# Hyena filter and maxout FFN: the products of the FFN beside the convolution in four column blocks of 32 in place of two of 64

## The chip, the cores and the metric

The kernel runs on one core of a Trainium2 chip. The time is the device time of one execution in microseconds; the kernel before took 2205.84 us, the median of three runs (2205.76 to 2206.69). The engines are called as the profile calls them: PE (TensorE, matrix products), PEld (PE's loads of the stationary operand), DVE (VectorE), ACT (ScalarE), POOL (GpSimd) and SP (SyncE, which issues DMAs).

## The reference

Two blocks follow one another, all in float32.

```
# hyena filter: x, v [4, 12544, 128], pos_emb [12544, 64], w1 [64, 64], w2 [64, 128]
h_filt = (np.maximum(pos_emb @ w1, 0.0) @ w2) * np.exp(-0.01 * pos)[:, None]
Uf = np.fft.rfft(x * v, n=2 * S, axis=1)
Hf = np.fft.rfft(h_filt, n=2 * S, axis=0)
y = x * np.fft.irfft(Uf * Hf[None, :, :], n=2 * S, axis=1)[:, :S, :]
# maxout FFN on the 50176 rows of y: moe_w1, moe_w2, moe_w3 [128, 768], moe_w_out [768, 128]
h = np.maximum(np.maximum(y @ moe_w1, y @ moe_w2), y @ moe_w3)
out = h @ moe_w_out
```

## The kernel before

The long convolution is done as a Fourier transform in two steps, with tables of constants: the 12544 positions are 98 blocks of 128, and a transform over the blocks (90 frequencies, `N1`) is followed by one within a block. Channels or positions lie on the partitions, and all of these transforms are matrix products on PE. The product with the filter's spectrum is element by element, on DVE, ACT and POOL; the way back is a second pair of transforms.

The work has three parts in time.

- First the filter, the weights and the convolution of batch 0, up to about 281 us of the span.
- Then the loop over `tiles[:LAST]`: 96 FFN tiles, 32 for each of the batches 0, 1 and 2. A tile is 392 positions (4 of the 128 within a block, by 98 blocks). Beside the tiles of batch b runs the convolution of batch b + 1; `conv_steps` lays its steps out over slots, six slots a tile, and `run` issues them at the end of each slot. This part ends at about 1792 us.
- Last the 32 tiles of batch 3, two at a time, with a scheme that needs fewer products, and no convolution beside them.

What belongs to a tile in the second part:

- `t_load` fetches the tile's spectrum from DRAM by DMA, `t_sums` forms two sums of it (L818, L820).
- `t_last`, the **last stage** of the inverse transform, makes 8 products of 49 columns, for 4 positions and the two halves of the 98 blocks: the sums `even` and `zt` in turn, times the table `f4p`, all into one bank. The bank is read by DVE, which multiplies with x (L839) into `gt`. It is called in one of the slots 2 to 4 of the tile before.
- `up` makes one of six chunks of 128 of the hidden layer: two products of 392 columns, `w_sb[1]` and `w_sb[2]` times `gt`, into two banks of `hps`. ACT takes the Relu of the first (L849), DVE the maximum with the second (L852). (The third matrix is folded in beforehand, into differences of the weights and a direct product `lin`.)
- `down` adds one chunk's product `wo_sb` times `hid` into the bank `ops`, two chunks after `up`; with the first chunk also `lin` times `gt`. After the sixth ACT copies the bank (L865) and POOL stores it by DMA (L867).

Beside them, of the convolution: `u_products` (L451, pieces of 49 rows by 64 columns, 90 columns wide) and `g_quarter` (L549 and L559, pieces of 64 rows by 64 columns, 128 columns wide). A `g_quarter` treats one step of the way forth and one of the way back, three steps apart, and between them stands a chain on the other engines: ACT's copy `eo` (L571), DVE's sums `cb` (L574), ACT's swap (L589, L590), DVE's products with the filter (L593, L598), POOL's add (L601) and DVE's `xs` (L605), which L559 reads. Those pieces are written out in the code and don't depend on the block's width.

The order on every engine is the order in the code (`manual_schedule`); buffers and data are waited for by semaphores.

`up`, `down` and `t_last` all send their products through one helper, `halves_mm` (L169 is its call of `matmul`). It cuts the stationary operand into blocks of `block[0]` columns, each of which fills as many partitions of the output, and sends the whole moving operand through each:

```
    block = [64]

    def halves_mm(out, lhsT, rhs, start, stop):
        w = block[0]
        for h in range(0, P, w):
            nc.tensor.matmul(out[h:h + w], lhsT[:, h:h + w], rhs,
                             start=start, stop=stop, skip_group_check=True)
```

In the trace every float32 matmul of the code stands as two records with a weight load each, here called two passes. A group's name gives rows and columns of the piece: `128*64` is 128 rows by a block of 64 columns, `90*64` the last stage's.

`block[0]` is 64 up to the end of the second part; the third part runs with 32 (its own products at L913 are cut in blocks of 32 by the code).

## Time and profile before

| | before |
|---|---|
| median of three runs | 2205.84 us (2205.76 to 2206.69) |
| the profiled execution | 2205.64 us |
| its span in the profile | 2203.9 us |
| granted clock of PE | 0.999 |
| busy in the span: PE, PEld, DVE | 2186.5, 1258.5, 1533.7 us |
| busy in the span: ACT, POOL | 1211.4, 1183.3 us |
| up products, 128*64 by 392 columns | 4616 records, 865.1 us busy |
| down products, 128*64 by 392 columns | 2304 records, 476.8 us busy |
| `lin` products, 128*64 by 392 columns | 384 records, 79.5 us busy |
| last stage, 90*64 by 49 columns, `zt` and `even` on `cps` | 1552 records each, 95.9 and 94.6 us busy |
| last stage of the third part, 90*32 by 49 columns | 960 records each, 24.1 and 24.2 us busy |

The busy time of a group is the time in which at least one of its records runs. Records overlap: blocks of columns work side by side, and the end of one pass lies over the start of the next, so the mean length of a record (494 ns for a wide one) is longer than the distance from pass to pass, and the distance between starts says what a pass costs.

### The profile page before, as it was taken

The numbers are of one execution on the slowest core, as the hardware profiler recorded it, in microseconds if no ns is written. First come the engines' busy times: TensorE is split into PE (matmuls) and PEld (weight loads), VectorE is DVE, ScalarE is ACT, GpSimd is POOL, SyncE is SP. The second block draws the span as 40 slices with busy tenths as digits, with TensorE's granted clock in tenths as the row PEclk, the third lists the DMA queues.
The fourth block names the chain that finished last, engine by engine and source line by source line (L and its number), as shares of the span: only waits on it lengthen the run. The fifth ranks groups of instructions, "written<-read, shape, count | busy, mean of one in ns | idle before, by whom it ended". The sixth has DMA issues, their size and how long they took to land.

```text
span 2203.9 us, 77207 instructions
## 1 busy us (share of the span) xinstructions
PE 2186.5 (99%) x31655; PEld 1258.5 (57%) x31655; DVE 1533.7 (70%) x3292; ACT 1211.4 (55%) x2223; POOL 1183.3 (54%) x1580
## 2 busy tenths in 40 slices
PE   9999999999999999999999999999999999999998
PEld 8988855555555555555555455555555545555565
DVE  5688966678888766668888766668878745454443
ACT  3699845466666555466666555456666522222222
POOL 1166568545544667535455566534545326666665
PEclk9999999999999999999999999999999999999999
DMA  8789999879999899789999899879999622222221
GB/s 200 184 262 318 302 181 206 170 196 247 248 245 246 209 189 178 155 193 243 245 245 251 212 193 175 171 172 244 242 251 241 179 75 59 65 71 69 59 59 24
DMA packets 491270, 411.62 MB, mean 187 GB/s; under 512 B 289379, under 2 KB 407901, under 8 KB 490917
## 3 DMA queue, kind: packets, MB, share of 16 engines
q1 hardware_dynamic: 443495, 274.33, 57.5%
q0 software_dynamic: 45936, 130.43, 20.9%
q8 instruction: 249, 4.08, 0.8%
q10 hardware_dynamic: 1486, 1.93, 0.4%
q14 instruction: 104, 0.85, 0.1%
HBM read 262.85 MB, written 84.68 MB: 158 GB/s over the span
## 4 chain that ended last, share of the span: by engine, by line
PE 93%; DVE 2%; POOL 2%; issue 1%; DMA 0%; ACT 0%; POOLq 0%; ACTq 0%; DVEq 0%
PE hps L169 46%; PE ops L169 20%; PE ops L913 6%; PE cps L169 4%; PE cps L549 3%; PE cps L451 3%; PE ps L178 3%; PE cps L559 3%; PE ps L169 2%; POOL xt L640 1%; PE last L169 1%; DVE ab L647 1%; PE ps L393 1%; DVE xs L639 1%; POOL specH L640 1%
## 5 line engine op out<-in xcount | busy, mean ns | idle before, releaser
L169 PE MATMUL hps<-gt,w_sb 128*64 128x392 f32 (+1 forms) x7672 | 1151.8, 494 | 1.8 <-DVE hid L852 1.0
L849 ACT ACTIVATE hid<-hps 128x392 f32<-128x392 f32 x768 | 382.4, 498 | 745.2 <-PE hps L169 726.9
L169 PEld LDWEIGHTS hps<-gt,w_sb 128*64 128x64 f32 (+1 forms) x7672 | 413.7, 126 | 454.5 <-issue 415.9
L852 DVE TENSOR_TENSOR hid<-hid,hps 128x392 f32<-128x392 f32 x768 | 428.5, 558 | 339.9 <-PE hps L169 321.4
L169 PE MATMUL ops<-hid,wo_sb 128*64 128x392 f32 x2304 | 476.8, 492 | 0.0
L601 POOL TENSOR_TENSOR cb<-cb,xs 128x512 f32<-128x512 f32 x135 | 178.2, 1320 | 358.3 <-DVE xs L598 349.8
L169 PEld LDWEIGHTS ops<-hid,wo_sb 128*64 128x64 f32 x2304 | 165.7, 137 | 213.5 <-issue 213.5
L574 DVE TENSOR_TENSOR cb<-cps,eo 128x512 f32<-128x512 f32 (+1 forms) x288 | 175.2, 650 | 78.0 <-ACT eo L571 76.9
L867 POOL DMA_DIRECT2D out_dram<-ot x96 | 77.1, 803 | 263.6 <-ACT ot L865 247.3
L589 ACT ACTIVATE xs<-cb 32x512 f32<-32x512 f32 x270 | 169.5, 628 | 21.9 <-DVE cb L574 13.1
L590 ACT COPY xs<-cb 32x512 f32<-32x512 f32 x270 | 166.3, 616 | 3.1
L605 DVE TENSOR_TENSOR xs<-cb 128x256 f32<-128x256 f32 x270 | 148.3, 598 | 7.3 <-POOL cb L601 7.3
L431 ACT COPY uT<-turned 113x512 uint16<-113x512 uint16 x180 | 125.9, 770 | 1.9 <-DMA turned<-planes 1.7
L388 POOL TENSOR_TENSOR ut<-ut 128x392 f32<-128x392 f32 x90 | 92.8, 1032 | 43.1 <-DMA ut<-in_vr_dram 42.9
L582 POOL DMA_DIRECT2D zd<-cb x135 | 93.8, 695 | 39.9 <-DVE cb L574 36.8
L169 PEld LDWEIGHTS cps<-f4p,even 90*64 90x64 f32 x1552 | 87.2, 138 | 35.9 <-issue 33.1
L777 POOL DMA_DIRECT2D xT<-in_x_dram x172 | 101.4, 605 | 4.6 <-DVE ab L647 3.1
L473 DVE TENSOR_TENSOR low<-high,cps 128x180 f32<-128x180 f32 x186 | 54.7, 336 | 68.9 <-ACT high L463 68.9
L938 POOL DMA_DIRECT2D out_dram<-o x120 | 72.6, 610 | 45.6 <-DVE o L931 44.5
L169 PE MATMUL cps<-f4p,zt 90*64 90x49 f32 x1552 | 95.9, 222 | 0.0
L415 POOL COPY planes<-ut 128x392 uint16<-128x392 uint16 x180 | 94.9, 561 | 0.0
L169 PE MATMUL cps<-f4p,even 90*64 90x49 f32 x1552 | 94.6, 220 | 0.0
(173 smaller groups left out, 3306.1 us busy)
## 6 DMA issues: line engine op xcount, KB each, us to landing
ht<-hd SPq DMA_DIRECT2D x264, 256.0 KB, 6.8
wt<-wq_const POOLq DMA_DIRECT2D x144, 256.0 KB, 5.6
zd<-cb POOLq DMA_DIRECT2D x135, 256.0 KB, 5.1
zt<-zd SPq DMA_DIRECT2D x384, 90.0 KB, 3.8
sq<-spec SPq DMA_DIRECT2D x528, 64.0 KB, 5.9
ut<-in_xr_dram SPq DMA_DIRECT2D x128, 196.0 KB, 4.0
ut<-in_vr_dram SPq DMA_DIRECT2D x128, 196.0 KB, 4.3
wt<-wt_const SPq DMA_DIRECT2D x90, 256.0 KB, 5.1
```

Source lines behind the costliest of these rows:

```text
L169: nc.tensor.matmul(out[h:h + w], lhsT[:, h:h + w], rhs, start=start, stop=stop, skip_group_check=True)
L415: nc.gpsimd.tensor_copy(w[:, h, :, :, 0:HB], a[:].bitcast(U16).rearrange("p s (m e h) -> p h s e m", e=2, h=2)[:, h])
L431: nc.scalar.copy(uts[u][0:HR, 8 * (u % 2):8 * (u % 2) + 8].rearrange("n s r t -> n (s r t)").bitcast(U16).rearrange("n (s r t h) -> n h s ...
L574: nc.vector.tensor_tensor(out=cb[:, a, lo:hi], in0=ps[:, lo:hi], in1=eo[:, lo:hi], op=op)
L589: nc.scalar.mul(xs[at:at + 32], xt[at + 32:at + 64], -1.0)
L590: nc.scalar.copy(xs[at + 32:at + 64], xt[at:at + 32])
L601: nc.gpsimd.tensor_tensor(out=xts[g], in0=xts[g], in1=xs[:], op=ALU.add)
L605: nc.vector.tensor_tensor(out=ab[:, q], in0=y[:, 0], in1=y[:, 1], op=(ALU.subtract, ALU.add)[q])
L777: eng.dma_start(xT[c * NG:(c + 1) * NG].rearrange("d i p n -> d (i p) n"), x[:, 4 * i:4 * i + 8, c, b, :])
L849: nc.scalar.activation(h[:], pa[:, 0:N], Relu)
L852: nc.vector.tensor_tensor(out=h[:], in0=h[:], in1=pb[:, 0:N], op=ALU.max)
L913: nc.tensor.matmul(ps[32 * q:32 * q + 32, 0:H2], w[:, m:m + 32], rhs[:, H2 * c:H2 * c + H2], start=start, stop=True, skip_group_check=True)
```

## The change

The width is set to 32 before the loop over the 96 tiles, not after it. So `up`, `down` and `t_last` send four blocks of 32 columns in the second part, too, each with its own weight load, where they sent two of 64. `t_last` runs 98 times in this loop, as it also makes the first two tiles of batch 3; `up` 577 times with the first chunk of batch 3; `down` for all 576 chunks, and `lin` 96 times. Products of the convolution, buffers, the other engines' instructions and the order of everything stay as they are. Line numbers between the two places rise by one.

```diff
             besides.setdefault((b - 1) * NT * NF + s, []).extend(steps)
+    block[0] = 32
     for n, (b, i) in enumerate(tiles[:LAST]):
         if i == 0:
             plan, pairs_from = plans[b]
...
     for l in late:
         down(*l)
     conv.close()
-    block[0] = 32
```

## The prediction

> **What bounds the kernel now.** I read the page first, then the busy time by stage, then the waits of PE inside the stage that the change touches.

> ```profile
> PE 2186.5 (99%) x31655; PEld 1258.5 (57%) x31655; DVE 1533.7 (70%) x3292; ACT 1211.4 (55%) x2223; POOL 1183.3 (54%) x1580
> ...
> PE 93%; DVE 2%; POOL 2%; issue 1%; DMA 0%; ACT 0%; POOLq 0%; ACTq 0%; DVEq 0%
> ```

> PE (TensorE) is busy 99% of the span and holds 93% of the chain that ended last. By stage (columns: PE, PEld, DVE, ACT, POOL, granted clock, DMA share, GB/s):

> ```profile
> 281.00:1792.00 1511.00, 1507.93 (x17676) 783.34 (x17672) 1122.33 (x2389) 892.27 (x1629) 799.71 (x1099) 1.00 0.94 210
> 1792.00:2203.90 411.90, 405.95 (x8178) 233.63 (x8176) 198.20 (x366) 105.79 (x224) 265.38 (x313) 1.00 0.23 58
> ```

> The first row is the stage of the change: FFN tiles of three batches beside the convolution of the next. The second is the last batch, which already uses blocks of 32; so one trace holds both block widths, at the same clock. PE's waits in the first stage:

> ```profile
> PE hps L169 <- DVE hid L852: 1.0, 1, 1.0
> PE hps L169 <- DVE gt L839: 0.7, 1, 0.7
> PE cps L559 <- DVE xs L605: 0.5, 2, 0.3
> ```

> Some 3 us in 1511: the stage is as long as PE's own work, and what the pieces of a product cost is what counts.

> **The last stage (t_last), 98 tiles.** Its products are 49 columns wide. With blocks of 64 (timeline of PE; start, length, instruction, count):

> ```profile
> 1206.35 0.27 PE L169 MATMUL cps<-f4p,even 90*64 90x49 f32 x4
> 1206.45 0.29 PE L169 MATMUL cps<-f4p,zt 90*64 90x49 f32 x4
> ...
> 1207.15 0.29 PE L169 MATMUL cps<-f4p,zt 90*64 90x49 f32 x4
> 1207.27 1.50 PE L169 MATMUL hps<-gt,w_sb 128*64 128x392 f32 x8
> ```

> With blocks of 32, in the last batch:

> ```profile
> 1854.71 0.27 PE L169 MATMUL last<-f4p,even 90*32 90x49 f32 x8
> 1854.80 0.27 PE L169 MATMUL last<-f4p,zt 90*32 90x49 f32 x8
> ...
> 1855.33 0.26 PE L169 MATMUL last<-f4p,zt 90*32 90x49 f32 x8
> 1855.42 0.83 PE L169 MATMUL hps<-gt,w_sb 128*32 128x392 f32 x8
> ```

> Eight products take 1207.27 - 1206.35 = 0.92 us by two blocks of 64 and 1855.42 - 1854.71 = 0.71 us by four of 32; the trace's starts in ns have medians of 0.920 (98 stages) and 0.706 (30 stages). One product is sent as two records for each block, 4 against 8, so the 32-wide pieces are twice as many and still quicker: 0.115 us a product becomes 0.088. [...] 96 tiles of three batches and the first two of the fourth get their last stage in this loop: 98 x 0.214 = **21.0 us less**. All of it is on PE, so on the path.

> [...]

> **The wide products.** Up and down products (392 columns) go from 4 records to 8. At 64, two ups and a down run 1204.37 to 1206.35, 0.66 us a product; at 32, 1859.72 to 1861.70 holds two ups and two half-wide products of the last batch (0.33 each), again 0.66 a full one. Median from pass to pass is 329 ns in both widths. Nothing saved, nothing added: **0**. The doubled weight loads lie under the products: the PEld rows below show 0.13 us of loading in each 0.33 at 32, 0.14 at 64; without that cover each would cost what the returns show, 0.02 to 0.05. ACT and DVE read the same banks in as many instructions; no DMA, SP or POOL instruction changes.

> **The weight loads after a change of shape.** When PE returns from the convolution's 64 x 64 pieces it starts empty, and the second load of the first up cannot hide (timeline of PEld):

> ```profile
> 1211.26 0.20 PEld L169 LDWEIGHTS hps<-gt,w_sb 128*64 128x64 f32 x4 [0.17 <-issue]
> 1211.65 0.14 PEld L169 LDWEIGHTS hps<-gt,w_sb 128*64 128x64 f32 x2 [0.19 <-issue]
> 1211.98 0.14 PEld L169 LDWEIGHTS hps<-gt,w_sb 128*64 128x64 f32 x2 [0.18 <-issue]
> ...
> 1792.13 0.16 PEld L169 LDWEIGHTS hps<-gt,w_sb 128*32 128x32 f32 x8 [0.61 <-DVE hid L852]
> 1792.49 0.13 PEld L169 LDWEIGHTS hps<-gt,w_sb 128*32 128x32 f32 x4 [0.20 <-issue]
> ```

> The second pass follows 0.39 us after the first, where 0.33 is usual (0.380 against 0.329 in ns); at the trace's one change into blocks of 32 (1792.13) it follows after 0.36 (0.353). So 0.027 less at each return. The order of work in the trace shows 118 visits to the convolution in this stage (72 of its products at L549 and L559, 46 of its transforms at L451), each with one return: 118 x 0.027 = **3.2 us less**. After a last stage the second pass is 15 ns late at 64 and 5 ns at 32; 95 such: **0.9 us less**. The one change from 64 to 32 at 1791.7 goes (0.431 against 0.329): **0.1 us less**.

> **The changes of shape themselves** (236, two a visit) stay as many, but are now from 128 x 32 to 64 x 64, which the trace doesn't show. Nearest rows, by starts in ns: 128 x 64 to 64 x 64 costs 0.100 and back 0.110; 128 x 98 to 98 x 64 and 128 x 64 to 128 x 32 cost 0.100; between 128 x 98 and 64 x 41, where rows and columns change at once, 0.095 to 0.100. I take no difference, as the last of these is the nearest in kind, with 12 ns either way on one half as bound (118 x 0.012 = 1.4 us). One more thing: after a return four blocks start 7 ns apart, so the last ends 20 ns after the first instead of 7, until a last stage closes them up again; the next change waits for it. Between 0 and 118 x 0.013 = 1.5; I take **1.0 us more**.

> **What is late next.** PE arrives earlier at the convolution's products, which read xs (DVE, L605). The chain behind it (ACT copies, DVE sums, POOL's add, L605) is in part of fixed length: from 482.83, where the visit ends, to 494.69 those engines hand over almost without a pause. Comparing L605's second half with the first pass that uses that group, visits leave 0.8 to 3 us, 0.2 to 0.5, 0.07 to 0.08, or, where no last stage lies between two visits, -0.09 to -0.02; down to -0.09 no pause of PE is seen, since the second half is read two passes later. About 57 of the gaps between visits hold one last stage and shrink by 0.24. If the chain didn't move at all, the visits at 0.08 would fall to -0.16 and lose some 0.07 us (about 10 of them, 0.7 us), the pause of 0.43 us at the end of the first two convolutions would grow by up to 0.24 each (0.5), and the dozen at -0.09 to -0.02 would lose the 0.03 of their return (0.3). Bounds: nothing, and 57 x 0.24 = 13.7; I take **1.5 us more**, by the measured slack.

> **The sum**: -21.0 - 3.2 - 0.9 - 0.1 + 1.0 + 1.5 = -22.7 us. The profiled execution took 2205.64 us (span 2203.9), 0.2 below the median of 2205.84; so 2182.9 on it and about 2183 for the median, 1.0% faster.

> **Rivals.**
> (a) The convolution's chain takes the gain back: nothing behind L605 moves with PE, and each gap gives up its 0.24. Then 13.7 in place of 1.5 is lost: 2195. For it: 11.9 us of nearly unbroken work between two visits. Against: that chain starts from PE's own visit, and most gaps have over 0.24 us to spare. 0.05.
> (b) A change of row and column size together is paid twice, 0.10 more on each of 236: +23.6, and the gain is gone, 2206.6, no difference. For it: the pair isn't in the trace. Against: the changes between 128 x 98 and 64 x 41 at the single price. 0.04.
> (c) Slower: under a DMA share of 0.94 (0.23 where the 32-wide stage was seen) the pieces don't overlap, and each costs what a 64-wide one does, 0.1175 / 4 = 0.029 us. The 784 products then take 8 x 0.029 = 0.235 us, not 0.1175: +92, less the 4 saved at the returns, plus 2.5: about 2296. It decides from about 0.015 us a piece, where the gain is gone. For it: twice the instructions have to come in while DMA is busy, 64 pieces more a tile. Against: up to 281 us the kernel ran 5807 matmul records (20.7 a us) at a DMA share of 0.86, where the changed stage would have 17676 + 10440 in about 1490 us (18.9 a us), and the convolution's 64 x 64 pieces, four side by side, keep 109 ns a pass at the full DMA load. 0.03. [...]
> That the change does nothing is excluded: the pieces of all three kinds go by the one helper, and the program's PE instructions change from 64 to 32 columns throughout this stage.

> **The numbers.** The forecast's mechanism has 0.88; its own range is 2179.2 (no stall, no skew, 1.4 off for the changes of shape) to 2190.5 (skew 1.5, half the bound of the stalls, 1.4). That holds 8 in 10 by itself, so the range is 2179 to 2191. Faster: forecast and (a), 0.93; about 0.2% (4.4 us) is what a measurement of this kernel can tell from no change. Same: (b), 0.04. Slower: (c), 0.03.

> **What would show it.** The groups of 90*64 pieces in this stage give way to 90*32 ones in twice the number, and a last stage to 0.71 us. The stage from 281 to 1792 ends near 1769, the last batch keeps its 412 us. The second pass after a return comes at 0.36. PE's wait for L605 stays below 2 us in sum; if it is 10, (a) is right. If the last pass before a visit and its first are more than 0.43 apart, (b); if the eight products take over 0.9 us, (c). Wide passes other than 329 ns would break the sum at the term I set to nothing.

## The result and the profile after

The changed kernel is slower: 2230.55 us, the median of four runs (2227.61 to 2234.29), against 2206.27 (2205.76 to 2207.26) of the kernel before on the same chip. The ratio is 1.0108 with a 95% interval of 1.0096 to 1.0119. The profiled execution took 2230.39 us, its span 2228.6.

The page's rows of engines and of the chain, and the one of PE's instruction queue, which is new to the reading (transfers, MB, share):

```profile
PE 2180.8 (98%) x42095; PEld 1234.7 (55%) x42095; DVE 1536.5 (69%) x3292; ACT 1213.0 (54%) x2223; POOL 1186.8 (53%) x1580
...
q8 instruction: 331, 5.42, 1.1%
...
PE 92%; DMA 3%; issue 2%; DVE 1%; ACT 1%; SPq 0%; ACTq 0%; POOL 0%; DVEq 0%; POOLq 0%
```

PE has 10,440 matmul records more, as foreseen, and yet 6 us less busy time (2186.5 before): the saving is there, and PE stands still for longer than it saved. (Of the chain's 3% of DMA, more than half lies ahead of the changed stage.) By stage, the changed one and the third part:

```profile
281.00:1815.00 1534.00, 1502.40 (x28172) 726.16 (x28167) 1124.59 (x2388) 894.23 (x1629) 803.40 (x1099) 1.00 0.95 207
1815.00:2228.60 413.60, 407.72 (x8204) 268.68 (x8196) 198.89 (x368) 106.27 (x225) 265.11 (x313) 1.00 0.23 59
```

Before, PE was idle for 3 us in the changed stage; now it is for 1534.00 - 1502.40 = 31.6. The last part is as it was. PE's waits in the changed stage:

```profile
PE hps L169 <- issue: 10.1, 6, 3.1
PE cps L549 <- issue: 6.1, 7, 1.6
PE cps L451 <- issue: 4.7, 2, 2.7
PE cps L559 <- issue: 3.7, 4, 1.5
PE cps L549 <- DMA sq<-spec: 1.5, 1, 1.5
PE cps L549 <- DVE hid L852: 1.2, 1, 1.2
...
PE cps L559 <- DVE xs L605: 0.5, 2, 0.2
```

Some 26 us of the idle time are "issue": PE waits for no semaphore that the profile shows. Two waits are new, for `sq` and for `hid`; what they are is said below. The wait for `xs`, which the prediction gave 1.5 us, has not moved.

**The part that came as forecast.** A last stage now, on PE's timeline:

```profile
1021.48 0.27 PE L169 MATMUL cps<-f4p,even 90*32 90x49 f32 x8
1021.57 0.27 PE L169 MATMUL cps<-f4p,zt 90*32 90x49 f32 x8
...
1022.10 0.27 PE L169 MATMUL cps<-f4p,zt 90*32 90x49 f32 x8
1022.19 1.50 PE L169 MATMUL hps<-gt,w_sb 128*32 128x392 f32 x16
```

That is 0.71 us, as in the last batch, at a DMA share of 0.95.

**What a pause looks like**, in the middle of a transform of the convolution:

```profile
426.53 0.84 PE L169 MATMUL ops<-hid,wo_sb 128*32 128x392 f32 x8
427.30 0.69 PE L451 MATMUL cps<-f1e,uT 49*64 49x90 f32 x23
430.66 1.91 PE L451 MATMUL cps<-f1e,uT 49*64 49x90 f32 x41 [2.67 <-issue]
```

23 of 64 pieces run, then nothing for 2.67 us, and the profile shows no semaphore that is waited for. The DMA records give the reason. PE's instructions come over queue q8, in 331 transfers of 16 KB (5.42 MB / 331). The trace holds 84,190 products and weight loads of PE and some 600 semaphore instructions, 256.2 for each of the 331 transfers: a transfer is a block of 256 instructions, 64 bytes each (16,384 / 256).

I counted PE's instructions in the program's order (four for each matmul of the code, and the semaphore instructions) up to each pause. The 13 longest of the changed stage all begin at the same place of 256, wherever in the work that is (0.79 to 0.82 of a block; the number depends on where the count begins, what matters is that it is the same each time), and all end 1.3 to 1.7 us after a q8 transfer has ended (here the transfer ran from 428.04 to 429.09). At none of the stage's 222 borders between blocks does PE go on sooner than 1.2 us after the end of the transfer that belongs there. So in these pauses PE stands at the border of an instruction block whose successor hasn't come.

Two of the 13 are the waits that the page puts down to `sq` and `hid`: they begin at such a border, too, and end 1.58 and 1.41 us after a transfer, though for `sq` the trace doesn't exclude that its data were late as well. One block is fetched ahead: by the array's time a transfer starts between 1.6 us before PE comes to the border before and 6.5 us after, in the median 1.6 us after.

Against each other, in us, worked out from the trace (time of a block: from border to border on PE; delay: from a border to the end of the next block's transfer, and 1.35 for what follows it, by the 1.3 to 1.7 above; how the semaphore instructions are counted in shifts single figures by up to half a microsecond):

| stage | time of a block: least, median | delay: median, a tenth over, longest |
|---|---|---|
| before, changed stage | 7.2, 10.6 | 3.3, 5.5, 7.6 |
| before, third part (blocks of 32, DMA share 0.23) | 4.0, 6.3 | 2.0, 3.3, 3.9 |
| after, changed stage | 3.6, 6.6 | 4.3, 7.0, 9.2 |

Before, even the shortest block lasted about as long as the longest delay, and in this stage nothing was seen of it. After, the two overlap. The transfer itself hardly differs (a median of 1.17 us in the changed stage, 1.09 in the third part before); what differs is how late it starts.

**The account.** I compared each stretch of equal work with the time that the fastest tenth of its kind takes, and summed the excess: 2.6 us before, 47.4 after. From the first wide product of the loop to the first narrow one of the third part it is 1521.8 us before and 1545.2 after: +23.4 = +44.8 of pauses - 21.4 of savings. In that excess lies a second thing. After four of the five longest pauses (2.24 to 3.61 us from start to start) PE's granted clock was halved for 3.41 us; the one of 2.95 us, up to 1012.85, was followed by the full clock. The first of the four:

```profile
330.25:331.67 1.42, 1.42 (x31) 0.91 (x35) 0.00 (x0) 0.46 (x1) 0.56 (x2) 1.00 1.07 245
331.67:335.08 3.41, 3.41 (x28) 1.09 (x21) 2.01 (x7) 0.50 (x1) 1.80 (x2) 0.50 1.27 170
335.08:340.00 4.92, 4.92 (x64) 1.94 (x60) 2.90 (x9) 3.39 (x7) 3.47 (x6) 1.00 1.04 229
```

The last column but two is the clock: 1.00, 0.50, 1.00. Wide passes at half the clock take 0.65 us in place of 0.33. The four stretches begin at 331.67, 430.66, 597.91 and 942.66 us, whole multiples of 3.413 us apart (29, 49 and 101). Half of 3.41 us, four times, is at most 6.8 of the 44.8 (one of the four began 0.44 us before its pause ended). The rest is pauses; of those the idle time of 31.6 us shows only what lies beyond the modelled ends of the last records. Counted another way, the 22 gaps of over 0.5 us between starts at block borders alone come to some 31 us.

### The profile page after: what moved, and what is told of

Its sections match the earlier page's. It is cut to its first block, busy times and chain, and to the rows that moved or that the text cites. A ratio compares the mean times of both kernels' runs of the same rounds, so it can differ in the third digit from the quotient of the medians.

```text
span 2228.6 us, 98087 instructions
## 1 busy us (share of the span) xinstructions
PE 2180.8 (98%) x42095; PEld 1234.7 (55%) x42095; DVE 1536.5 (69%) x3292; ACT 1213.0 (54%) x2223; POOL 1186.8 (53%) x1580
## 3 DMA queue, kind: packets, MB, share of 16 engines
q8 instruction: 331, 5.42, 1.1%
## 4 chain that ended last, share of the span: by engine, by line
PE 92%; DMA 3%; issue 2%; DVE 1%; ACT 1%; SPq 0%; ACTq 0%; POOL 0%; DVEq 0%; POOLq 0%
PE hps L169 45%; PE ops L169 19%; PE ops L913 6%; PE cps L549 3%; PE ps L169 3%; PE cps L169 3%; PE cps L451 3%; PE ps L178 3%; PE cps L559 3%; PE sps L1135 2%; PE last L169 1%; PE gps L1110 1%; PE ps L393 1%; DMA ht<-hd 1%; PE ps L355 1%
## 5 line engine op out<-in xcount | busy, mean ns | idle before, releaser
L169 PE MATMUL hps<-gt,w_sb 128*32 128x392 f32 x12288 | 1172.9, 494 | 12.0 <-issue 10.1
L852 DVE TENSOR_TENSOR hid<-hid,hps 128x392 f32<-128x392 f32 x768 | 428.6, 558 | 367.2 <-PE hps L169 350.4
L169 PEld LDWEIGHTS hps<-gt,w_sb 128*32 128x32 f32 x12288 | 404.8, 110 | 476.0 <-issue 426.4
L169 PE MATMUL ops<-hid,wo_sb 128*32 128x392 f32 x4608 | 497.5, 494 | 0.0
L169 PEld LDWEIGHTS ops<-hid,wo_sb 128*32 128x32 f32 x4608 | 156.0, 110 | 227.1 <-issue 224.4
L605 DVE TENSOR_TENSOR xs<-cb 128x256 f32<-128x256 f32 x270 | 148.6, 598 | 7.3 <-POOL cb L601 7.3
L549 PE MATMUL cps<-sq,wt 64*64 64x128 f32 x2160 | 90.3, 277 | 8.8 <-issue 6.1
L169 PEld LDWEIGHTS cps<-f4p,even 90*32 90x32 f32 x3104 | 76.2, 109 | 39.2 <-issue 30.4
L593 DVE TENSOR_TENSOR cb<-cb,ht 128x512 f32<-128x512 f32 x135 | 92.0, 682 | 3.1 <-ACT xs L590 3.1
```

The source lines that it names most:

```text
L169: nc.tensor.matmul(out[h:h + w], lhsT[:, h:h + w], rhs, start=start, stop=stop, skip_group_check=True)
L549: nc.tensor.matmul(ps[64 * a:64 * a + 64, at:at + D], w[64 * r:64 * r + 64, k, a, :], t[64 * r:64 * r + 64, k, :, a], start=(k == 0), stop ...
L605: nc.vector.tensor_tensor(out=ab[:, q], in0=y[:, 0], in1=y[:, 1], op=(ALU.subtract, ALU.add)[q])
L852: nc.vector.tensor_tensor(out=h[:], in0=h[:], in1=pb[:, 0:N], op=ALU.max)
```

## The experiments

Theory 1 is the supply of instructions, as above. Theory 2 is the rival: something in the width of 32, in the array or in the change between 128x32 and 64x64, that pauses now and then. Ratios are to the kernel before on the same chip, with 95% intervals.

**s1_cut_columns.** As many instructions for the wide products, with blocks of 64.

```diff
-        for h in range(0, P, w):
-            nc.tensor.matmul(out[h:h + w], lhsT[:, h:h + w], rhs,
+        for at in range(0, n, c):          # c = n // 2 for n > 256 in the loop
+            for h in range(0, P, w):
+                nc.tensor.matmul(out[h:h + w, at:at + c], lhsT[:, h:h + w], rhs[:, at:at + c],
```

> Blocks stay 64 wide; instead every wide product of the loop (up, down, lin) is sent in two halves of 196 moving columns, so PE has as many matmul and load instructions for them as with four blocks of 32 (some 25.0 thousand records of matmuls in the stage against 17.7 before and 28.2 in the changed kernel), at the same array time but for 1 to 3 ns a pass (up to 9 us). Theory 1, instruction supply (PE's instructions come in blocks of 256 by DMA, one block ahead; where PE runs through 256 sooner than the next block lands, it stands still): pauses named issue come back, all at the same place of the 256, some 20 to 40 us; time 2225 to 2255. Theory 2, the width itself (blocks of 32 pause under load, or the change of shape between 128x32 and 64x64 sometimes takes microseconds): no such pauses; 2206 to 2216.

Measured 2220.75 us, 1.0065 (1.0048 to 1.0082). The stage is 15.1 us longer: some 9 from the shorter passes (7304 records, about 1.2 ns each) and 6.0 of pauses (excess 8.6 against 2.6). PE's longest wait is again

```profile
PE cps L563 <- issue: 3.1, 3, 1.4
```

(L563 is L559 here.) The three pauses over 0.95 us begin at 0.80 of a block and end 1.4 to 1.6 us after a transfer. So pauses come without any block of 32, against theory 2, but fewer than I gave theory 1, and the time lies between the two ranges: a block still lasted 4.8 us at the least and 7.3 in the median, against delays with a median of 3.8.

**s5_cut_four.** The same with four pieces of 98 columns.

> Blocks stay 64 wide, every wide product of the loop is sent in four pieces of 98 moving columns: some 39.6 thousand matmul records in the stage, at the array's own time but for 2 to 4 ns a piece (30 to 55 us). A block of 256 instructions then lasts some 5 us of wide products, all the time, where the changed kernel's lasted 4.0 at the least and 6.8 in the median. Theory 1 (instruction supply), with the delays from one block's border to the next block's use as the changed kernel shows them (median 4.3, a quarter over 5.9, a tenth over 7.0 us): 0.3 to 0.6 us for each of some 310 blocks, 90 to 190 us on top, 2320 to 2450, all pauses at the place 0.80 of a block. Theory 2 (something in the width of 32): no pauses, 2235 to 2265.

Measured 2383.79 us, 1.0800 (1.0780 to 1.0819), within the range for theory 1. Blocks lasted 4.2 us (a twentieth of them less) to 5.2 (median); the delay's median is 4.7.

```profile
PE hps L173 <- issue: 49.8, 44, 4.5
PE ops L173 <- issue: 26.9, 22, 3.3
PE cps L173 <- issue: 11.0, 8, 2.2
```

All 57 pauses over 0.95 us begin at 0.80 to 0.82 of a block. The width is 64 throughout the stage. This settles it for theory 1: denser instructions made the pauses, with no block of 32 in the stage.

**s2_after_light and s3_before_light.** The changed kernel and the kernel before with fewer DMAs.

```diff
     def h_load(g, n):
+        if g >= 4:                          # and q_load in the same way
+            for x in range(n):
+                hts[g + x] = held["h", g // 2 % 2][:, x]
+            return
```

> The changed kernel without most of two kinds of DMA beside the FFN: of the loads of ht and sq only the first two pairs of each convolution are done and their data used again (the output's values are not the reference's), 93 of 317 MB in the stage. Theory 1: with the DMA engines less busy a block of instructions lands sooner, the pauses go to under 10 us, and the forecast gain shows: 15 to 24 us faster than the kernel before with the same loads left out (s3), about 2183. Theory 2: nothing changes for the pauses; some 25 us slower than s3, 2225 to 2232.

> The kernel before with the same loads of ht and sq left out as in s2 (the output's values are not the reference's). Both theories: PE sets the time here and had no pauses, so 2202 to 2207.

Measured 2197.66 us, 0.9961 (0.9946 to 0.9975), and 2206.72 us, 1.0000 (0.9991 to 1.0009). With the DMA share of the stage down,

```profile
281.00:1815.00 1534.00, 1521.83 (x28712) 733.07 (x28707) 1140.55 (x2418) 903.60 (x1650) 818.57 (x1114) 1.00 0.64 146
```

the delay's median falls from 4.3 to 3.1 us, the excess from 47.4 to 18.9, and the change becomes a gain of 9.1 us over s3. The kernel before doesn't care for the load. The stages differ by 1515.8 - 1523.0 = -7.2 = +16.7 of pauses - 23.9 of savings: the forecast saving is real, also here. But s3 ran the first 6 us of the stage at half the clock (0.50 from 285.05 to 291.88 us), which cost it 1.7 us that the kernel before and s2 didn't pay; without that the saving is 22.2, near the 21.4 above. The gain is less than I expected, as the pauses at the transforms (L451) stay, two of the three long ones at the same places.

**s9_after_no_sq and s10_after_no_ht.** One of the two kinds left out at a time.

> The changed kernel without most loads of sq alone (as in s2; the output's values are not the reference's): 31 MB of 317, but some 130 thousand of the stage's 385 thousand packets. Theory 1 as it stands after s2 and s5: a block of instructions comes late by what the DMA engines have before it. If the number of packets counts: most of s2's gain, 2200 to 2212. If the bytes count: a third of it, 2215 to 2224.

> The changed kernel without most loads of ht alone (as in s2; the output's values are not the reference's): 62 MB of 317 in packets of 2 KB, some 31 thousand of 385 thousand. If the bytes count: two thirds of s2's gain, 2206 to 2214. If the number of packets counts: little, 2222 to 2230.

Measured 2207.36 us, 0.9994 (0.9985 to 1.0003), and 2200.06 us, 0.9962 (0.9948 to 0.9976); delays with a median of 4.0 and 3.4 us, excess 24.1 and 15.0. s9 lies in the range for packets; s10, which should then have changed little, lies below both of its ranges and gains as much as s2 (0.9961). So neither bytes nor packets alone decides. That a delay costs only what it exceeds the block's time by, so that the first relief takes most of the cost, fits both but isn't shown by itself. In these versions of the changed kernel the delay's median follows the DMA share of the stage: 4.3, 4.0, 3.4 and 3.1 us at 0.95, 0.86, 0.77 and 0.64; that the share alone isn't the rule shows in s6 below and in the kernel before (3.3 at 0.94).

**s8_after_spread.** The changed kernel with the loads of `ht` and `sq` spread over slots.

```diff
-                        at(s - 3, 0, h_load, g, min(2, NK - g))
+                        for k in range(4):
+                            at(s - 4 + k, 0, h_load, g, min(2, NK - g), (k,))
```

> The changed kernel with the loads of ht and sq spread over more slots: the four of a pair of ht one slot each in place of all in one, those of sq four and four two slots apart. Same bytes, same PE. Theory 1, if a block waits behind bursts in the DMA engines' queues: pauses go from 45 us to some 25, 2205 to 2215. Theory 1, if it is the load as such (a share of 0.95): no change, 2226 to 2234. Theory 2: no change.

Measured 2239.71 us, 1.0150 (1.0131 to 1.0170): worse than the change. The delay's median is 4.5 us, the excess 58.8, 3.9 us of it a new wait for `sq` itself. So spreading these loads doesn't bring a block sooner, and their burst isn't what makes it late.

**s6_third_part_loaded.** The kernel before, with loads added where the width is 32 already.

```diff
+            extra(step)      # one load of hd, 256 KB, or two of xr and vr, 196 KB each, in turn
```

> The kernel before, with added DMA loads in its third part alone, which runs in blocks of 32 and had no pauses at a DMA share of 0.23: at each of its 192 steps a load of 256 KB, or two of 196 KB, into tiles that nobody reads. PE's instructions don't change. Theory 1: a block there lasts 4.0 to 6.3 us, and the next one took 1.2 to 3.9 us to come; under load it takes longer, and pauses named issue appear at 0.80 of a block, 10 to 40 us: 2216 to 2246. Theory 2 in the form that only the change between 128x32 and 64x64 pauses: none, since the third part has no such change: 2205 to 2208. Waits of PE for zt or x would be the loads' own queue and are counted apart.

Measured 2207.63 us, 0.9999 (0.9990 to 1.0008): no pause, against my expectation. The DMA share of the part went from 0.23 to 0.82 and the rate from 58 to 214 GB/s, but the delay's median only from 2.0 to 2.8 us and the longest to 4.8, beside blocks of at least 4.0. So a rate of 214 GB/s by itself didn't make instructions late enough here; in the changed stage it is 207 at a share of 0.95, with POOL's queue, transposes and small packets in it, and the delay is 4.3. Which of these makes the difference stays open.

**s4_last_32.** Only the last stage at 32.

```diff
+        was, block[0] = block[0], 32
         for s in range(4):
             for a in range(2):
                 halves_mm(...)
+        block[0] = was
```

> Only the last stage goes to blocks of 32; up and down keep 64. Both theories: 98 last stages save 0.21 us each (21.0), but each now has a change of shape on both sides, 0.10 in, 0.11 out and 0.05 for the second load: plus 25; together plus 4. Theory 1: the stage has only 3136 more matmul records, but 128 of PE's instructions in 0.7 us at each last stage: pauses of 0 to 10 us, 2208 to 2220. Theory 2: the pauses belong to 32-wide blocks or to their change of shape, which is now twice a tile more often: pauses of 20 us or more, 2230 and above.

Measured 2220.14 us, 1.0059 (1.0044 to 1.0074), just above the range for theory 1 and well under theory 2's. The stage is 12.1 us longer: 6.9 of pauses (excess 9.5) and 5 from the changes of shape, which eat the saving as worked out.

**s7_32_where_quiet and s11_32_longer.** 32 only in some tiles.

```diff
+        block[0] = 32 if i >= NT - 2 or b and i * NF < pairs_from - 8 else 64
```

> Blocks of 32 only in 24 of the 96 tiles: those beside the first steps of the second and third convolution, and the last two of each batch, where the changed kernel showed no pause of 0.55 us; 64 in the others, with four or five changes between. Theory 1: 24 x 0.24 = 5.8 us saved, 0.6 for the changes, a pause or two: 2200 to 2203 against 2206. Theory 2 makes no pause there either, so this one only tells whether the forecast gain can be had.

> As s7, with blocks of 32 in more tiles: up to the slot at which the second convolution's second half begins, and in the third batch seven tiles longer, 33 tiles in all. Theory 1: 33 x 0.24 = 7.9 us saved, 0.6 for the changes, and 2 to 5 us of pauses, as the steps of the convolution's second half are reached: 2200 to 2205 against 2206. The gain is no larger than that of s7 where the pauses eat the added tiles.

s7: 2204.03 us, 0.9983 (0.9974 to 0.9991), 11 runs: of the versions that compute the reference's values the one that beats both kernels, by 0.17%. In microseconds it lies above its range, but that range was set against 2206, and the kernel before took 2208.04 on this chip: 4.0 us are gained, where 3 to 6 were forecast. In the profiled execution, the fastest of the 11, the stage is 4.1 us shorter, and of "issue" 0.4 us is left:

```profile
PE hps L169 <- DVE hid L852: 1.0, 1, 1.0
PE hps L169 <- DVE gt L839: 0.7, 1, 0.7
PE cps L559 <- DVE xs L605: 0.5, 2, 0.3
PE cps L451 <- issue: 0.4, 1, 0.4
```

s11: 2210.90 us, 1.0013 (1.0002 to 1.0024): above the range. Nine more tiles, beside the second half of the convolution, bring an excess of 16.1 (in a profiled execution that took 4.5 us longer than the median) and lose it all again.

## Why the prediction was wrong

**The terms of the sum** held. A last stage takes 0.704 to 0.706 us (forecast 0.706). The second pass after a return is 353 ns after the first, in the median of 118 returns (forecast 353). A change of shape costs the same 0.100 from the last piece (422 ns before and after) and is met 14 ns later by the four blocks' skew (forecast up to 13). The wait for L605 stayed at 0.5. With these, -21.2 - 3.2 - 0.9 - 0.1 + 1.7 = -23.7 would have been the result; -21.4 and -22.2 are what the accounts of the changed kernel and of s2 leave when the pauses are taken out.

**The step that failed** is the "nothing" for the doubled instructions of the wide products, and the argument against rival (c). There the prediction had the right place, that twice the instructions have to come in while DMA is busy, and the wrong mechanism and price: pieces that don't overlap, at 92 us, decided by the rate of the last stage. The pieces overlap as in the last batch. What is lost is whole pauses at the borders of instruction blocks, most of them at wide products and convolution pieces: 44.8 us with the clock, where the prediction had 0.

The evidence set against it was a mean: 20.7 matmul records a us in the first 281 us at a DMA share of 0.86, against 18.9 in the changed stage. The mean says nothing on a border. There a block's time stands against one delay. In the first part the longest delay is some 5.5 us; in the changed stage it was 7.6 before the change already. The trace of before had both numbers: a shortest block of 7.2 us and a longest delay of 7.6. To halve the first was to walk into the second. Reading the starts and ends of the q8 transfers would have shown it; I read only the waits, in which a cost that is still covered doesn't appear.

And that first part was no clean evidence: one such pause stands in it, in the middle of a run of equal pieces (the list of waits from 0 to 281 us in the kernel before, then PE's timeline):

```profile
PE ps L355 <- issue: 0.9, 2, 0.6
...
19.99 3.03 PE L355 MATMUL ps<-w_sb,specH 64*41 64x64 f32 x115
23.61 0.58 PE L355 MATMUL ps<-w_sb,specH 64*41 64x64 f32 x13 [0.58 <-issue]
```

PE goes on at 23.61, at the same place of 256 as after the change, and 1.40 us after the end of a q8 transfer (21.25 to 22.21). The block before it had lasted 4.2 us.

**The rivals.** (a) didn't happen: the chain behind L605 leaves PE its time. (b) didn't: the change from 128x32 to 64x64 has the single price (0.100). (c) named the sign, not the cause: its own mark, eight products of the last stage in over 0.9 us, did not show. At a DMA share of 0.95 the 64 pieces start in 0.704 us, 11 ns apiece.

What stays open: which DMA traffic makes a block late (s6, s9 and s10 rule out the plain rate and either kind alone), and some 2 us between the forecast and the measured savings.

## What to carry to other kernels

The edit left the array time of PE's wide products alone (329 ns a pass in both widths) and doubled their instructions, and it was not free: 44.8 us of pauses stood against 21.4 saved. Before such an edit, compare the shortest time that the engine takes for one instruction block with the longest delay of such a block's transfer, stage by stage, not their means; here they were 7.2 and 7.6 us. The list of waits, 3 us in all, showed nothing of a cost that was just covered; look for how much cover is left before you halve it. The short pause named issue amid equal pieces, as at 23.61 us here, was the sign that it had run out somewhere. Where the dense version pays, use it only in the stretches where blocks still come in time, as s7 does (0.17% faster).
